# First MLP layer: a fourth pair of raw weight buffers, and the end of its first stage in written order

## The chip, the cores and the metric

The kernel runs on one core of a Trainium2 chip. The core has five engines with a queue of instructions each: PE (TensorE, matrix products), DVE (VectorE), ACT (ScalarE), POOL (GpSimd) and SP (SyncE, which here only issues transfers); POOL issues transfers too. The metric is the device time of the kernel in microseconds (us), the median of several runs. A change of under 0.2% of it, about 2 us, is not told from no change here.

## The reference, cut to what matters

The program works on x of 2048 tokens by 640 channels: four blocks one after the other, a spectral filter, a token MLP, the same filter again, the same MLP again.

```
def _B_ref(x, w1, b1, w2, b2):                 # w1 2048 x 1728, w2 1728 x 2048
    h = _layernorm(x, axis=-1)
    u = jnp.einsum("bsd,sf->bdf", h, w1) + b1
    u = _gelu(u)
    y = jnp.einsum("bdf,fs->bds", u, w2) + b2
    return y transposed to (b, s, d)

x = A_x
x = x + _A_ref(_layernorm(x), A_w_r, A_w_i)    # rfft2, times w_r + i w_i, irfft2
x = x + _B_ref(_layernorm(x), B_w1, B_b1, B_w2, B_b2)
x = x + _A_ref(_layernorm(x), A_w_r, A_w_i)
x = x + _B_ref(_layernorm(x), B_w1, B_b1, B_w2, B_b2)
```

## The kernel before, in words

`run` calls, twice, the spectral block (`a1`, `a2`) and an MLP: `b1st` the first time, `b2nd` the second. The change lies in `b1st` (lines 929 to 1166), the first MLP, and in one number set in `setup` (line 134).

**Precision.** Products are in float16 with each operand split into a high and a low part. A weight tile `raw` (float32) gives `wh` (ACT, a scaled copy) and `wl` (DVE, the rest); `h` is `hh` and `hl`, `u` is `uh` and `ul`. A product is three: high by high, low by high, high by low. Before a weight tile can be split its scale must be known: ACT reads the tile once and sums squares (`scan1`, the `junk<-raw` instructions), DVE reduces (`sqb`), PE adds over the partitions with a product by ones (`total`, a one-column matmul into `ps`), and some six one-column DVE operations make a power of two (`scale1`; `step(m)` runs the next piece of it).

**First stage.** A loop over `ft` = 0 to 13 (line 1008); the text calls one turn product `ft`. Each makes a tile of u, 128 features by 640 channels, from 16 blocks `j` of h; its weights are tile `m = ft`, taken in the order `SEQ`. From `ft` = 2 on a product is 96 matmuls of 320 columns, `both` (line 997). After it comes the gelu (lines 1060 to 1075): ACT writes `t` and `q` from the accumulator, DVE makes `q`, ACT takes the tanh, DVE writes `uf[i]`, the float32 u. `uh` and `ul` are made from `uf` by `usplit` (line 980, two DVE operations), which needs `su`, the scale of u, set by `scale_u` in product 11 at `j` = 8. Before the change the first six parts are spread over product 12, the next six over product 13, and the last two follow at the end (lines 1057 to 1059, 1076 and 1077).

**Second stage.** A loop over 16 rows `j` (line 1105), weight tiles m = 14 to 29. A row is 82 matmuls over the 14 tiles of u in the order `SEQ`; the last six of them read `uh[12]` and `ul[12]`, the last tile made. The result is added to a row of x (`xt`, loaded by `load`), written back, normalised and folded for the next spectral block, whose first products (`a0_s1`, `ps<-tM,fh` and `ps<-tM,fl`) lie between the rows.

**Weight pipeline.** While product or row m runs, these are issued (m counted through both stages): `wload(m + 3)` on SP, two transfers of half a tile each; `wstore(m)` and, in the first stage, sums of tiles (`wsum`, `wssplit`), kept for the second MLP and issued from POOL; `wsplit(m + 1)` (ACT `wh`, DVE `wl`, two halves); `scan1(m + 3)` and the steps of its scale. The raw tiles go in turn into `nr` = 3 pairs of buffers: `wr[max(m - 2, 0) % nr]`, in the pools `wraw`, `wr` and `wr2` (line 866). So the load of tile m + 3 goes into the buffers of tile m and waits until `wl` of m and the sums with it have read them. The split parts have two sets of buffers (`wp[m % 2]`), so `wh` of m + 2 waits until the product of m is done.

**Order.** A planner puts the instructions of each engine in an order of its own, by its own estimates of when each can start; the engines then run in that order. While `self.pin` is true, an instruction that goes through the wrappers of `Pin` (line 49: DVE, ACT, POOL's computing, PE) is tied behind the one written before it on the same engine. Transfers issued by `nc.sync` and `nc.gpsimd` are not tied. In `b1st` only lines 939 to 949 and the last row of the second stage (lines 1124 to 1153) are pinned before the change.

**Memory.** Pools lie on two stacks from the two ends of the on-chip memory, left and right; a tile put where a closed pool lay waits for the last reader of the tiles it covers. After the first stage `uf`, `b1`, `h` and `ha` are closed and the pools of the second stage's spectral tables (`tD`, `tM`, `tS2`, `tI2`) and rows (`xt`) are opened there.

## Time and profile before

| what | value |
|---|---|
| median of 3 runs | 1017.25 us (1016.85 to 1018.95) |
| the profiled execution's own time | 1017.07 us |
| its span, first to last instruction | 1015.3 us |
| PE busy | 969.4 us, 95% |
| DVE busy | 781.8 us, 77% |
| ACT busy | 576.5 us, 57% |
| POOL busy | 300.0 us, 30% |
| mean granted PE clock | 0.979 |

Times in the profile are counted from the first instruction. Almost all compute instructions carry line 59, the line of the `Pin` wrapper that issues them, so they are told apart by the names of their tiles: `ps<-hl,wh` is a matmul with `hl` moving and `wh` as weights. A row of a timeline has the start, the time from start to end of the group, the engine, the line, the operation, output and inputs, the shape and the count; in square brackets stand the idle time before it and what ended that. A row of waits has the waiting engine and tile, the releaser, the total in us, how often, and the longest. In tables by stretch each engine has its busy time and, in brackets, its instruction count; PEclk is the granted clock of PE as a share of full speed, and the last two columns are the share of time the DMA engines were busy and the GB/s they moved.

The first stage of the first MLP lies from about 184 us (first products of `both_high`) to 367 us, its second stage from 367 to about 567 us.

### The profile page before, as it was taken

The numbers are of one execution on the slowest core, as the hardware profiler recorded it, in microseconds if no ns is written. First come the engines' busy times: TensorE is split into PE (matmuls) and PEld (weight loads), VectorE is DVE, ScalarE is ACT, GpSimd is POOL, SyncE is SP. The second block draws the span as 40 slices with busy tenths as digits, with TensorE's granted clock in tenths as the row PEclk, the third lists the DMA queues.
The fourth block names the chain that finished last, engine by engine and source line by source line (L and its number), as shares of the span: only waits on it lengthen the run. The fifth ranks groups of instructions, "written<-read, shape, count | busy, mean of one in ns | idle before, by whom it ended". The sixth has DMA issues, their size and how long they took to land.

```text
span 1015.3 us, 20992 instructions
## 1 busy us (share of the span) xinstructions
PE 969.4 (95%) x8235; PEld 721.2 (71%) x8235; DVE 781.8 (77%) x1493; ACT 576.5 (57%) x890; POOL 300.0 (30%) x502
## 2 busy tenths in 40 slices
PE   4889999999999999999999799999999999999998
PEld 3778777677777667777777688776777777677776
DVE  7978978988777784666666689789965557998885
ACT  5857668687666455555553377685643454544531
POOL 6937857412212201222222277574000000000000
PEclk9599999999999999999999999999999999999999
DMA  7865356557657546464423455365444446755411
GB/s 232 279 185 164 115 178 219 206 187 255 236 195 250 186 124 246 139 193 146 126 89 117 126 181 181 105 229 204 159 156 164 145 142 228 245 177 190 153 45 53
DMA packets 67259, 176.45 MB, mean 174 GB/s; under 512 B 7996, under 2 KB 15320, under 8 KB 67160
## 3 DMA queue, kind: packets, MB, share of 16 engines
q1 hardware_dynamic: 59384, 146.92, 45.1%
q0 software_dynamic: 7776, 28.20, 7.5%
q8 instruction: 64, 1.05, 0.4%
q14 instruction: 35, 0.29, 0.1%
HBM read 127.24 MB, written 47.84 MB: 172 GB/s over the span
## 4 chain that ended last, share of the span: by engine, by line
PE 36%; DVE 13%; ACT 6%; POOL 3%; issue 3%; DMA 2%; SPq 0%; ACTq 0%; DVEq 0%; POOLq 0%
PE ps L59 36%; DVE wl L59 3%; DMA xt<-x 2%; DVE st L59 2%; DVE xt L59 1%; POOL eo L59 1%; DVE f L59 1%; ACT wh L59 1%; ACT xt L59 1%; ACT z L59 1%; DVE s1l L59 1%; ACT junk L59 1%; POOL xt L59 1%; DVE Yl L59 1%; DVE S L59 1%
## 5 line engine op out<-in xcount | busy, mean ns | idle before, releaser
L59 PEld LDWEIGHTS <-wh 128*128 128x128 f16 x2602 | 251.9, 98 | 103.6 <-issue 5.0
L59 PEld LDWEIGHTS <-wl 128*128 128x128 f16 x1610 | 157.5, 98 | 66.0 <-DVE wl L59 2.8
L59 PE MATMUL ps<-ul,wh 128*128 128x320 f16 x448 | 133.9, 301 | 0.6 <-DVE ul L59 0.6
L59 PE MATMUL ps<-uh,wl 128*128 128x320 f16 x448 | 133.9, 301 | 0.1
L59 PE MATMUL ps<-uh,wh 128*128 128x320 f16 x416 | 124.8, 300 | 1.6 <-DVE s L59 1.6
L59 PE MATMUL ps<-hl,wh 128*128 128x320 f16 x496 | 102.2, 299 | 0.9 <-DVE hl L59 0.9
L59 PEld LDWEIGHTS <-wo 128*128 128x128 f16 x756 | 73.9, 98 | 29.4 <-DVE wo L59 0.8
L59 DVE SCALAR_TENSOR_TENSOR wl<-raw,s,wh 128x896 f16<-128x896 f32 (+2 forms) x64 | 75.0, 1176 | 12.9 <-ACT wh L59 12.7
L59 ACT ACTIVATE junk<-raw 128x896 bf16<-128x896 f32 (+1 forms) x60 | 59.5, 991 | 44.2 <-DMA raw<-w 44.0
L59 POOL TENSOR_TENSOR r<-v,mh 128x1 f32<-128x1 f32 x64 | 36.4, 569 | 158.4 <-DVE nm L59 149.0
L59 PE MATMUL ps<-tDi,Yh 128*128 128x322 f16 x320 | 71.3, 300 | 0.2
L59 DVE TENSOR_TENSOR f<-eo 128x256 f32<-128x256 f32 (+1 forms) x124 | 39.1, 368 | 40.7 <-POOL eo L59 40.1
L59 ACT ACTIVATE wh<-raw,s 128x896 f16<-128x896 f32 (+2 forms) x68 | 67.2, 1010 | 2.3 <-DVE s L59 1.6
L59 POOL TENSOR_TENSOR xt<-xt,ec 128x320 f32<-128x320 f32 x64 | 52.5, 842 | 34.2 <-DVE xt L59 34.0
L59 ACT ACTIVATE z<-xt,nb,r 128x640 f32<-128x640 f32 x31 | 28.5, 919 | 57.6 <-POOL z L59 45.3
L59 PE MATMUL ps<-ph,tS 128*128 128x321 f16 (+2 forms) x288 | 58.5, 286 | 1.3 <-DVE tb L59 1.3
L59 PE MATMUL ps<-u,wo 128*128 128x320 f16 x420 | 59.0, 299 | 0.5 <-DVE wo L59 0.5
L59 DVE BATCH_NORM_STATS2 st<-xt 128x6 f32<-128x320 f32 x126 | 55.3, 480 | 5.2 <-DMA xt<-x 4.5
L59 PE MATMUL ps<-hha,wh 128*128 128x320 f16 x288 | 58.1, 299 | 0.9 <-DVE wh L59 0.9
L59 POOL TENSOR_TENSOR eo<-z 128x320 f32<-128x320 f32 x62 | 53.3, 881 | 17.0 <-ACT z L59 15.1
L59 PE MATMUL ps<-tM,f 128*128 128x128 f32 x160 | 39.5, 426 | 19.6 <-DVE f L59 19.6
L59 PE MATMUL ps<-tDi,Yl 128*128 128x322 f16 x192 | 55.7, 299 | 1.7 <-DVE Yl L59 1.7
(251 smaller groups left out, 2376.6 us busy)
## 6 DMA issues: line engine op xcount, KB each, us to landing
xt<-x SPq DMA_DIRECT2D x79, 320.0 KB
raw<-w SPq DMA_DIRECT2D x32, 512.0 KB
w<-w SPq DMA_DIRECT2D x48, 321.0 KB
x<-xt SPq DMA_DIRECT2D x47, 320.0 KB
raw<-w SPq DMA_DIRECT2D x32, 448.0 KB
raw<-w2z SPq DMA_DIRECT2D x32, 448.0 KB
w1S<-sp POOLq DMA_DIRECT2D x20, 512.0 KB, 3.7
out<-xt SPq DMA_DIRECT2D x15, 320.0 KB
```

Source lines behind the costliest of these rows:

```text
L59: i = f(*a, **k)
```

## The change

There are now four pairs of raw buffers: `nr` is 4, a pool `wr3` is opened beside `wr` and `wr2`, tiles 3, 4 and 5 are loaded ahead of the loop, and product or row m loads tile m + 4. The scan of a tile stays where it was written.

From the end of product 11's matmuls to the end of the first stage (`ft >= NFT - 3`) the instructions are pinned in written order: the gelu of product 11, all of products 12 and 13 with their gelus, and the last parts of u.

The 14 parts of u (`usplit`, now taken in turn by `nextu`) are spread anew: two beside each of the last three gelus (one after `q`'s ACT write, one after the tanh), three in each of the products 12 and 13 (`j` = 6, 9, 12), two at the end.

```
-        self.second, self.nr = False, 3
+        self.second, self.nr = False, 4
...
-        self.wr[1:3] = (self.push(a, side=self.sp) for a in ("wr", "wr2"))
+        self.wr[1:] = (self.push(a, side=self.sp) for a in ("wr", "wr2", "wr3"))
...
-        for m in (3, 4):
+        for m in (3, 4, 5):
             self.wload(m)

         def ahead(m, w):

-            if m + 3 < NFT + NJ:
-                self.wload(m + 3)
+            if m + 4 < NFT + NJ:
+                self.wload(m + 4)
...
+        todo = iter(SEQ)
+
+        def nextu():
+            i = next(todo)
+            usplit(i, uf[i])
...
-                    if ft >= NFT - 2 and 1 < j < 14 and j % 2 != ft % 2:
-                        i = SEQ[(j - 2) // 2 + 6 * (ft - NFT + 2)]
-                        usplit(i, uf[i])
+                    if ft >= NFT - 2 and j in (6, 9, 12):
+                        nextu()
+            self.pin = ft >= NFT - 3
             dup, i = ft == 1, SEQ[ft]
...
             T.activation(q, pv, AF.Square, scale=c1, bias=bb)
+            if ft >= NFT - 3:
+                nextu()
             V.scalar_tensor_tensor(q, q, 1.0 / GC, t, op0=ALU.add, op1=ALU.mult)
             T.activation(q, q, AF.Tanh, scale=GS * GC)
+            if ft >= NFT - 3:
+                nextu()
             V.scalar_tensor_tensor(uf[i], q, 1.0, t, op0=ALU.add, op1=ALU.mult)
-        for k in SEQ[12:]:
-            usplit(k, uf[k])
+        nextu()
+        nextu()
+        self.pin = False
...
+        self.pop("wr3")
         self.pop("wr2")
```

## The prediction

> **What bounds the kernel now.** I read first how busy the engines are by stretch: the first stage from product 2 on, then the second stage once its first row is through.

> ```profile
> 207.00:367.00 160.00, 157.79 (x1171) 113.20 (x1169) 127.61 (x222) 105.63 (x139) 34.52 (x63) 1.00 0.63 216
> 382.00:557.00 175.00, 174.86 (x1415) 128.46 (x1414) 107.33 (x303) 89.77 (x131) 36.27 (x84) 1.00 0.47 148
> ```

> PE (first pair of numbers) is busy in 157.8 of 160 us and in 174.9 of 175. Only PE's gaps can be won. The waits of PE between 207 and 382 us are four:

> ```profile
> PE ps L59 <- DVE wl L59: 1.7, 1, 1.7
> PE ps L59 <- DVE s L59: 1.6, 1, 1.6
> PE ps L59 <- DVE ul L59: 0.6, 1, 0.6
> PE ps L59 <- DVE sqb L59: 0.5, 1, 0.5
> ```

> PE's timeline places the first three, and the windows give the clock beside them:

> ```profile
> 352.25 0.43 PE L59 MATMUL ps<-hl,wh 128*128 128x320 f16 x2
> 354.36 0.45 PE L59 MATMUL ps<-hha,wl 128*128 128x320 f16 x2 [1.67 <-DVE wl L59]
> ```
> ```profile
> 366.89 0.30 PE L59 MATMUL ps<-uh,wh 128*128 128x320 f16 x1
> ...
> 377.10 0.30 PE L59 MATMUL ps<-uh,wl 128*128 128x320 f16 x1
> 379.05 0.30 PE L59 MATMUL ps<-uh,wh 128*128 128x320 f16 x1 [1.65 <-DVE s L59]
> 379.97 0.43 PE L59 MATMUL ps<-ul,wh 128*128 128x320 f16 x1 [0.62 <-DVE ul L59]
> ...
> 383.23 0.30 PE L59 MATMUL ps<-ul,wh 128*128 128x320 f16 x1
> ```
> ```profile
> 352.00:354.00 2.00, 0.69 (x6) 0.28 (x3) 2.00 (x5) 0.00 (x0) 1.23 (x1) 1.00 0.11 47
> ```
> ```profile
> 380.00:382.00 2.00, 2.00 (x8) 1.14 (x8) 0.21 (x1) 0.79 (x1) 0.00 (x0) 0.50 1.04 426
> ```

> The 76 matmuls from 366.89 to 377.10 are 75 steps in 10.21 us, 0.136 us a matmul; a product of 96 is then 13.06 us. Product 13 stops after two pairs for its `wl` (354.36). The second stage begins at 366.89 and stops after 377.10 for the last tile of u, twice (for `uh`, which ended at 378.99, and for `ul`; the `s` named in the first wait is a small operation that ran just behind `uh`), and then runs at clock 0.50. Why is the last u late? The chain of waits, followed back from the end, passes there:

> ```profile
> 373.93 0.77 ACT t L59
> 374.70 0.79 ACT q L59
> 375.51 0.90 DVE q L59 x2
> 376.52 1.15 DVE wl L59
> 377.67 0.73 DVE uf L59
> 378.47 0.52 DVE uh L59
> 379.06 0.86 DVE ul L59
> ```
> ```profile
> 382.22 8.62 DMA xt<-x
> 390.86 0.84 ACT xt L59
> ```
> ```profile
> ACT junk L59 <- DMA raw<-w: 42.7, 21, 3.8
> ```
> ```profile
> 368.75 0.95 ACT L59 ACTIVATE junk<-raw 128x896 bf16<-128x896 f32 x1 [2.02 <-DMA raw<-w]
> ```

> Product 13 was done when 366.89 began, but ACT starts its gelu at 373.93: ACT goes in order, and ahead of `t` stand the scans of a later tile, waiting for their load (2.02 here; 42.7 between 207 and 382 us, up to 3.8 at once). SP issues such a load only when `wl` of an older tile has freed its buffer. So load, scan, `wh`, `wl`, load is a ring that runs just in time, and each gelu trails its product.

> **The parts, one by one.**

> *Fourth pair.* A tile is loaded one product (13.06 us) earlier against its scan. The longest wait, 3.8 us, fits three times over, so the 42.7 us on ACT go, and ACT can start a gelu when its product ends. Bytes and instructions stay; SP's loads are the same, each behind an older `wl`. The one new early load, tile 5, is behind tiles 3 and 4 in the same queue, and the DMA engines then stand idle:

> ```profile
> 202.00:204.00 2.00, 1.63 (x11) 1.06 (x11) 1.72 (x8) 0.59 (x1) 0.00 (x0) 1.00 0.00 0
> ```

> I cost it at nothing; if that cover is missing, tile 3's scale is later, and PE's wait for `sqb` (0.5, above) grows. That wait is the bound both ways: 0.5 won or about as much lost.

> *Parts of u moved.* In the middle of product 12 DVE ran parts back to back and only then `wl` of product 13:

> ```profile
> 350.45 1.67 DVE L59 SCALAR_TENSOR_TENSOR ul<-uf,su,uh 128x640 f16<-128x640 f32 x2
> 352.11 1.00 DVE L59 TENSOR_SCALAR uh<-uf,su 128x640 f16<-128x640 f32 x2
> 353.03 1.27 DVE L59 SCALAR_TENSOR_TENSOR wl<-raw,s,wh 128x1024 f16<-128x1024 f32 x1
> ```

> A part is (1.67 + 1.00)/2 = 1.34 us. In written order product 12's slot holds the gelu of product 11 with two parts, then both `wl` (`j` = 2 and 4), then three parts: 5 x 1.34 + q and uf 1.63 + two `wl` 2.5 = 10.8 us of DVE in 13.06. `wl` is done 1.56 (t and q, below) + 0.90 + 1.34 + 0.73 + 2.5 = 7.0 us into product 12, six before it is wanted. Won: 354.36 - (352.25 + 2 x 0.136) = 1.84 us.

> *The end of the stage.* Call T the end of product 13. DVE and ACT then need: t and q 1.56 (a part beside them), DVE q 0.90, a part 1.34 (longer than the tanh beside it), uf 0.73, two parts 2.68: the last u is ready at T + 7.2. PE asks for it after 76 matmuls, at T + 10.3. Both stops go: 379.05 - 377.24 = 1.81, and 379.97 - 379.19 = 0.78. With them goes the slow clock: 13 steps took 3.26 us from 379.97 to 383.23 where 13 x 0.136 = 1.77 would do; 1.49.

> What is late next? `wl` of row 1's tile: its buffer is free only at T, DVE has it done by T + 7.2 + 2 x 1.15 = T + 9.5 if all of it queues behind the parts, and row 1 starts after 82 matmuls, at T + 11.15. The small scale operations share the 1.65 left. Bounds: nothing, or a stop like the 1.84 above; I take nothing.

> *The pinned order.* Its added wait: PE's one-column sums, tied at `j` = 4 and 10, hold every matmul behind them until DVE has reduced a scan. Between 0 and the 0.5 of the `sqb` row; I take 0, since the scans no longer wait. On ACT the scans of product 13 stand ahead of its gelu, now for tiles loaded a product earlier. POOL's queue has one tied memset; nobody waits for it before row 0.

> **Does the second stage pass the gain on?** Its rows are nearly bound by a second thing:

> ```profile
> 405.31 0.30 PE L59 MATMUL ps<-uh,wh 128*128 128x320 f16 x1
> 513.34 0.30 PE L59 MATMUL ps<-uh,wh 128*128 128x320 f16 x1
> 525.55 0.30 PE L59 MATMUL ps<-uh,wh 128*128 128x320 f16 x1
> 537.76 0.30 PE L59 MATMUL ps<-uh,wh 128*128 128x320 f16 x1
> ```
> ```profile
> 520.07 1.03 ACT junk L59 x2
> ...
> 526.72 28.77 PE ps L59 x229
> ```

> From 405.31 to 513.34 PE makes nine rows of 12.00; the next two take 12.21. In the chain of waits no step is PE's from 377 to 526.72: it runs over ACT, DVE, POOL and transfers. Its second-stage part starts when the first `xt` lands (390.86), gains no time, and has caught PE up at 513: 2 x 0.21 = 0.42 lost. So PE's gain arrives only if the first `xt` comes earlier by as much. It was issued 2.3 us after the last `ul` (379.92) and landed 8.62 later. With T = 366.89 - 1.84 = 365.05 the last u is at 372.25, and by the same intervals `xt` lands at 383.2, 7.7 us earlier. That exceeds PE's gain, so the 0.42 goes too.

> Sum: 1.84 + 1.81 + 0.78 + 1.49 + 0.42 = 6.34 us. The profiled execution took 1017.07, its span 1015.3; it becomes 1010.7. The median, 0.18 above it, becomes 1010.9. Two microseconds, 0.2%, is about what can be told from no change.

> [...] The 1.84 gap left the clock at 1.00; 1.81 and 0.78, one matmul apart, were followed by 0.50. [...]

> **Rivals.**

> *One: the chain starts no earlier.* SP may still issue the loads of the second stage behind raw loads that wait for row 1's `wl`, which hangs on T. Before, `xt` landed 390.86 - 366.89 = 24.0 after T; kept, it lands at 389.0, 1.84 earlier, and the chain, which decides at the end, gives 1015.4. For it: the chain ran for eleven rows without PE. Against: it now has the last u 7.7 us earlier, and one raw tile less to wait for.

> *Two: the slow clock is not owed to the gap* and stays: 1010.9 + 1.49 = 1012.4. For it: the 1.84 gap did nothing. Against: 0.50 begins right behind the stop.

> *Three: something of the gain is eaten by the bounds above* (a stop of up to 1.84 at row 1, 0.5 at a sum, some of the chain): 1012 to 1014.

> *Four, slower: the rows get a longer chain.* The planner orders the second stage anew, since raw tiles come earlier; if one more scan (1.03, the `junk` step) comes to stand in each row's chain, eleven rows to 526 pay 11.3. Less 6 us of earlier start that is 5.3 slower, 1022.5. It decides from 0.73 us a row on. For it: the chain is already the slower of the two by 0.21. Against: scans stand in it already, as at 520.07, and have more freedom now.

> **Chances.** The forecast 0.53 (1010 to 1012.3), two 0.05, three 0.14, one 0.13, four 0.15. Faster by over 0.2% (below 1015.2): 0.53 + 0.05 + 0.14 = 0.72. Same: 0.13, rival one at 1015.4. Slower: 0.15. The range reaches from 1009.9 (the forecast less the `sqb` wait and as much again at the start) to 1017.0, past rival one, and leaves out rival four and a little below.

> **What would show it.** ACT's waits for `raw` near zero; `t` of product 13 within 1 us of its last matmul; no stop at the first `wl` of product 13 nor at the last `ul`; clock 1.00 through both stages; the first `xt` landed within 19 us of T; row spacing 12.0 to the end. I am wrong if PE gets new waits for `wl` in the second stage, or stops at a sum.

## The result and the profile after

The changed kernel took 1011.89 us (median of 5 runs, 1010.04 to 1012.57), the kernel before 1017.25 (median of 5, 1016.5 to 1018.95). The ratio is 0.9936, with a 95% interval of 0.9923 to 0.9948: 6.5 us faster, between 5.3 and 7.8 (the two medians differ by 5.4). The profiled execution took 1010.95 against 1017.07, its span 1009.1 against 1015.3. A second set of runs of the same two kernels (further down) gave 1012.70 against 1017.94, ratio 0.9955 [0.9938, 0.9972], 4.6 us faster.

The stretches first, as before: from product 2 on, then the second stage once its first row is through (busy time of PE, PEld, DVE, ACT and POOL, granted clock, share of DMA, GB/s).

```profile
207.00:365.00 158.00, 157.29 (x1169) 113.02 (x1167) 127.87 (x227) 108.20 (x144) 32.74 (x63) 1.00 0.64 223
380.00:551.00 171.00, 171.00 (x1395) 126.39 (x1393) 104.23 (x301) 86.05 (x123) 36.21 (x84) 1.00 0.44 141
```

PE is busy in 157.3 of 158 us and in all of 171.0. Its waits between 207 and 382 us, four in the kernel before, are one kind, and ACT's waits for raw tiles are about half of what they were:

```profile
PE ps L59 <- DVE sqb L59: 0.7, 2, 0.5
```
```profile
ACT junk L59 <- DMA raw<-w: 22.4, 12, 3.0
```

PE's timeline: the second stage begins 1.65 us earlier (366.89 before), the last part of u costs a step of 0.32 instead of 0.136, and the rows that started at 405.31, 513.34, 525.55 and 537.76 start here:

```profile
365.24 0.30 PE L59 MATMUL ps<-uh,wh 128*128 128x320 f16 x1
...
375.59 0.30 PE L59 MATMUL ps<-uh,wh 128*128 128x320 f16 x1
375.91 0.30 PE L59 MATMUL ps<-ul,wh 128*128 128x320 f16 x1
...
399.75 0.30 PE L59 MATMUL ps<-uh,wh 128*128 128x320 f16 x1
507.76 0.30 PE L59 MATMUL ps<-uh,wh 128*128 128x320 f16 x1
519.79 0.30 PE L59 MATMUL ps<-uh,wh 128*128 128x320 f16 x1
531.79 0.30 PE L59 MATMUL ps<-uh,wh 128*128 128x320 f16 x1
```

From 387.75 to 531.79 the rows are 12.00 to 12.03 apart. The chain of waits passes the end of the first stage as before, only earlier:

```profile
374.47 0.46 DVE uh L59
...
375.00 0.86 DVE ul L59
...
375.88 9.19 DMA xt<-x
...
385.10 0.84 ACT xt L59
```

ACT and DVE at the end of product 13 do not look as predicted:

```profile
364.51 0.95 ACT L59 ACTIVATE junk<-raw 128x896 bf16<-128x896 f32 x1 [2.83 <-issue]
...
365.58 0.95 ACT L59 ACTIVATE junk<-raw 128x896 bf16<-128x896 f32 x1
...
366.53 1.03 ACT L59 ACTIVATE wh<-raw,s 128x896 f16<-128x896 f32 x1
367.47 0.87 ACT L59 ACTIVATE t<-ps,b1s,c 128x640 f32<-128x640 f32 x1
```
```profile
367.59 1.15 DVE L59 SCALAR_TENSOR_TENSOR wl<-raw,s,wh 128x896 f16<-128x896 f32 x1 [1.79 <-PE ps L59]
...
370.41 1.15 DVE L59 SCALAR_TENSOR_TENSOR wl<-raw,s,wh 128x896 f16<-128x896 f32 x1
```

Two scans and a `wh` of later tiles stand ahead of `t`, which starts 2.2 us after the product's end, and two `wl` stand between the steps of the gelu on DVE. The first of these scans waits 2.83 us, for which this profile names no releaser. In run e7 (below) ACT has the same work here, and there it is named:

```profile
364.46 0.95 ACT L59 ACTIVATE junk<-raw 128x896 bf16<-128x896 f32 x1 [2.82 <-DVE sqb L59]
```

So this wait is for a sum on DVE and not for a load. By the count of scans it is the scan for row 1 (tile 18). The kernel keeps the sums of squares in two `sq` tiles in turn, so this scan can write only once `sqb` of tile 16 has read the one it needs, and the pin ties that `sqb` behind the parts of u in product 13. The link over `sq` is read from the kernel; no run changes it.

Where did the 6.2 us of span come from? Four distances cut it up. The first stage, from the last stop for `hl` near 203 us (202.94 before, 202.91 after) to T, the start of the second stage: 163.95 to 162.33, 1.62 won. From T to the twelfth row start counted from 405.31 and 399.75, called row 12 here and in the expectations: 170.87 to 166.55, 4.32 won. From there to the first product with `tD` behind the last row:

```profile
571.34 0.31 PE L59 MATMUL ps<-tD,s1h 128*128 128x160 f16 x2 [0.39 <-ACT s1h L59]
```
```profile
564.65 0.32 PE L59 MATMUL ps<-tD,s1h 128*128 128x160 f16 x2 [0.45 <-ACT s1h L59]
```

33.58 to 32.86, 0.72 won. From there to the end 443.96 to 444.45, 0.49 lost again. 1.62 + 4.32 + 0.72 - 0.49 = 6.17, and 0.03 from the start. In a second pair of profiles (a1 and a2 below) the same four distances give 0.46, 4.24, 1.11 and 1.83, and 1.41 from the start: only the 4.3 of the second stage repeats.

### The profile page after: what moved, and what is told of

It is laid out like the page before. It is cut to its first block, busy times and chain, and to the rows that moved or that the text cites. A ratio compares the mean times of both kernels' runs of the same rounds, so it can differ in the third digit from the quotient of the medians.

```text
span 1009.1 us, 20992 instructions
## 1 busy us (share of the span) xinstructions
PE 966.7 (96%) x8235; PEld 720.8 (71%) x8235; DVE 781.1 (77%) x1493; ACT 577.0 (57%) x890; POOL 297.9 (30%) x502
## 4 chain that ended last, share of the span: by engine, by line
PE 48%; DVE 22%; ACT 12%; POOL 8%; issue 6%; DMA 4%; SPq 0%; ACTq 0%; DVEq 0%; POOLq 0%
PE ps L59 48%; DVE wl L59 3%; POOL eo L59 3%; DVE f L59 3%; DMA xt<-x 2%; DVE st L59 2%; DVE xt L59 2%; ACT junk L59 2%; ACT z L59 2%; ACT wh L59 2%; POOL xt L59 2%; DVE s1l L59 1%; DVE Yl L59 1%; ACT xt L59 1%; DVE hl L59 1%
## 5 line engine op out<-in xcount | busy, mean ns | idle before, releaser
L59 PEld LDWEIGHTS <-wh 128*128 128x128 f16 x2602 | 251.4, 98 | 101.3 <-issue 3.1
L59 PEld LDWEIGHTS <-wl 128*128 128x128 f16 x1610 | 157.5, 98 | 62.2 <-issue 1.0
L59 PE MATMUL ps<-ul,wh 128*128 128x320 f16 x448 | 133.1, 299 | 0.0
L59 PE MATMUL ps<-uh,wl 128*128 128x320 f16 x448 | 133.1, 299 | 0.0
L59 PE MATMUL ps<-uh,wh 128*128 128x320 f16 x416 | 124.3, 299 | 0.0
L59 PE MATMUL ps<-hl,wh 128*128 128x320 f16 x496 | 102.3, 299 | 0.9 <-DVE hl L59 0.9
L59 PEld LDWEIGHTS <-wo 128*128 128x128 f16 x756 | 73.9, 98 | 29.4 <-DVE wo L59 0.8
L59 DVE SCALAR_TENSOR_TENSOR wl<-raw,s,wh 128x896 f16<-128x896 f32 (+2 forms) x64 | 75.1, 1177 | 22.5 <-ACT wh L59 19.6
L59 POOL TENSOR_TENSOR r<-v,mh 128x1 f32<-128x1 f32 x64 | 36.3, 567 | 162.1 <-DVE nm L59 152.6
L59 ACT ACTIVATE junk<-raw 128x896 bf16<-128x896 f32 (+1 forms) x60 | 59.5, 992 | 27.6 <-DMA raw<-w 24.4
L59 PE MATMUL ps<-tDi,Yh 128*128 128x322 f16 x320 | 71.3, 300 | 0.2
L59 ACT ACTIVATE wh<-raw,s 128x896 f16<-128x896 f32 (+2 forms) x68 | 67.1, 1010 | 6.0 <-DVE s L59 5.5
L59 DVE TENSOR_TENSOR f<-eo 128x256 f32<-128x256 f32 (+1 forms) x124 | 39.0, 368 | 40.6 <-POOL eo L59 40.1
L59 POOL TENSOR_TENSOR xt<-xt,ec 128x320 f32<-128x320 f32 x64 | 52.4, 841 | 34.0 <-DVE xt L59 33.9
L59 ACT ACTIVATE z<-xt,nb,r 128x640 f32<-128x640 f32 x31 | 28.5, 919 | 57.0 <-POOL z L59 45.2
L59 PE MATMUL ps<-ph,tS 128*128 128x321 f16 (+2 forms) x288 | 58.5, 286 | 1.3 <-DVE tb L59 1.3
L59 PE MATMUL ps<-u,wo 128*128 128x320 f16 x420 | 59.0, 299 | 0.5 <-DVE wo L59 0.5
L59 DVE BATCH_NORM_STATS2 st<-xt 128x6 f32<-128x320 f32 x126 | 55.3, 481 | 5.2 <-DMA xt<-x 4.5
L59 PE MATMUL ps<-hha,wh 128*128 128x320 f16 x288 | 58.1, 299 | 0.9 <-DVE wh L59 0.9
L59 POOL TENSOR_TENSOR eo<-z 128x320 f32<-128x320 f32 x62 | 53.3, 880 | 17.1 <-ACT z L59 15.1
L59 PE MATMUL ps<-tM,f 128*128 128x128 f32 x160 | 39.5, 426 | 19.6 <-DVE f L59 19.6
L59 PE MATMUL ps<-tDi,Yl 128*128 128x322 f16 x192 | 55.7, 299 | 1.5 <-DVE Yl L59 1.5
```

The costliest lines, as they stand in the source:

```text
L59: i = f(*a, **k)
```

## The experiments

Two theories at the start. **R**: the fourth pair did it, by loosening the ring of load, scan, `wh`, `wl` that holds up ACT. **O**: the order did it, the pinning and the new places of the parts. All runs in one table; the medians are over 5 to 12 runs, the ratio is to runs of the kernel before on the same chip (1017.81, 1017.47 and 1017.94 for the three groups of experiments), the distances are those of the profiled execution, and "xt" is when ACT takes the first `xt`, counted from T.

| run | median us | ratio [95%] | first stage | xt after T | row 12 after T | row 12 to `tD` | ACT's raw waits |
|---|---|---|---|---|---|---|---|
| before | 1017.25 | | 163.95 | 23.97 | 170.87 | 33.58 | 42.7 |
| a1, before again | 1017.42 | 1.0006 [0.9991, 1.0021] | 162.45 | 24.00 | 170.76 | 33.55 | 42.6 |
| after | 1011.89 | 0.9936 [0.9923, 0.9948] | 162.33 | 19.86 | 166.55 | 32.86 | 22.4 |
| a2, after again | 1012.70 | 0.9955 [0.9938, 0.9972] | 161.99 | 19.75 | 166.52 | 32.44 | 23.1 |
| e1, pair only | 1014.53 | 0.9967 [0.9955, 0.9979] | 162.33 | 22.83 | 169.35 | 32.79 | 40.3 |
| e2, order only | 1012.79 | 0.9953 [0.9939, 0.9967] | 162.11 | 20.95 | 167.76 | 33.53 | 31.8 |
| e3, no pin | 1014.47 | 0.9970 [0.9957, 0.9983] | 161.98 | 22.91 | 169.45 | 32.78 | 39.1 |
| e4, parts at old places | 1012.97 | 0.9953 [0.9940, 0.9967] | 161.99 | 22.64 | 170.67 | 32.23 | 23.8 |
| e5, last u 1.5 late | 1013.80 | 0.9969 [0.9959, 0.9980] | 162.43 | 19.62 | 168.12 | 32.23 | 22.5 |
| e6, last u 3.0 late | 1014.90 | 0.9980 [0.9965, 0.9995] | 162.26 | 20.55 | 168.75 | 32.24 | 24.5 |
| e7, xt later | 1012.19 | 0.9952 [0.9936, 0.9968] | 162.62 | 22.71 | 166.63 | 32.82 | 24.2 |
| e8, five pairs | 1013.61 | 0.9957 [0.9940, 0.9974] | 164.77 | 20.14 | 166.53 | 31.63 | 11.8 |
| e9, e1 with xt first | 1012.79 | 0.9956 [0.9942, 0.9971] | 162.50 | 15.82 | 167.54 | 32.23 | 42.6 |
| e10, after with xt first | 1010.50 | 0.9929 [0.9915, 0.9943] | 162.99 | 15.16 | 166.53 | 32.24 | 24.4 |

The intervals of e1 to e5 and a2 overlap, so the medians hardly rank the variants. The argument rests on the distances to row 12, of one profile each; in both kernels that were profiled twice, that distance repeated to 0.11 us.

### Which part of the change

**e1, the fourth pair alone** (the diff's pinning and `nextu` left out):

```
-        self.second, self.nr = False, 3
+        self.second, self.nr = False, 4
...
-            if m + 3 < NFT + NJ:
-                self.wload(m + 3)
+            if m + 4 < NFT + NJ:
+                self.wload(m + 4)
```

> The fourth pair of buffers alone; pins and parts of u as before. If the ring of load, scan, wh and wl is the cause (theory R), ACT's waits for raw tiles fall by half or more, t of product 13 starts within 3 us of the last matmul of that product, the 2.6 us of stops for the last u and the slow clock behind them go, and the second stage keeps 12.0 us a row: 1011 to 1013.5, the upper end if the parts still push wl of product 13 back by 1.8. If the order on the engines is the cause (theory O), the waits for raw tiles go too, but the cluster of parts still stands ahead of wl of product 13 and the last u stays late: 1014 to 1017.

ACT's waits for raw hardly fall, the stop at the first `wl` of product 13 is gone, the slow clock is not there (from T to the row at 402.08 it is 35.57 us, 38.42 in the kernel before and 34.51 in the changed one), and yet the kernel wins only 3 us. The rows say why:

```profile
ACT junk L59 <- DMA raw<-w: 40.3, 19, 4.6
```
```profile
389.34 2.38 ACT L59 ACTIVATE xt<-xt,b2s 128x640 f32<-128x640 f32 x3 [6.86 <-DMA xt<-x]
```
```profile
402.08 0.30 PE L59 MATMUL ps<-uh,wh 128*128 128x320 f16 x1
414.08 0.30 PE L59 MATMUL ps<-uh,wh 128*128 128x320 f16 x1
...
523.86 0.30 PE L59 MATMUL ps<-uh,wh 128*128 128x320 f16 x1
```

One row of 12.00, and then nine in 109.78 us, 12.20 each, which is the pace of the chain over ACT, DVE, POOL and transfers that the kernel before showed from 513 on. PE came to the second stage earlier, but the first `xt` landed at T + 22.8, and the chain caught PE up at the second of these rows. This is the prediction's rival one, nearly as it was worked out there (1015.4). Neither theory had all its signs right: `t` of product 13 starts 5.6 us after its product and the waits for raw stay, against R, and the late `wl` of product 13 that O expected is gone.

**e2, the order alone** (three pairs):

```
-        self.second, self.nr = False, 4
+        self.second, self.nr = False, 3
...
-            if m + 4 < NFT + NJ:
-                self.wload(m + 4)
+            if m + 3 < NFT + NJ:
+                self.wload(m + 3)
```

> The pinned order and the new places of the parts alone, with three pairs of buffers. Theory R: the scans still wait for their loads, in pinned order ahead of the gelus, so t of product 13 starts some 5 us or more after its product and the stops for the last u stay: 1015 to 1017. Theory O: wl of product 13 comes before the parts and frees the buffers early, the ring has slack in products 12 and 13 without a fourth pair: 1011 to 1012.5.

Most of the gain is there: 4.8 us by the ratio, with `t` of product 13 3.2 us behind its product. Small stops remain, and `xt` is 1.1 us later than in the changed kernel:

```profile
367.47 0.18 PE L59 MATMUL ps<-sqb,ones 128*128 128x1 bf16 x1 [0.39 <-DVE sqb L59]
376.53 0.30 PE L59 MATMUL ps<-ul,wh 128*128 128x320 f16 x1 [0.41 <-DVE ul L59]
```

With the fourth pair these go too; in the profiles that is 1.2 us at row 12 and 0.7 to 1.1 behind it, while the medians (1012.79 against 1011.89 and 1012.70) do not settle it.

**e3, the changed kernel without the pinning**:

```
-            self.pin = ft >= NFT - 3
```

> The changed kernel without the pin; four pairs and the new places of the parts stay. Theory R: the planner has what it needs, 1011 to 1012.5, no stop of PE above 0.5 between 207 and 380 us. Theory O: without the tie the planner runs the parts ahead of wl of product 13 or ahead of DVE's gelu operations again: a stop of 1 to 2 us, 1013 to 1016.

It ends where e1 does: raw waits 39.1, the first `xt` at T + 22.9, rows of 12.20 (and one of 13.02, in which PE stops for 0.32 and 0.35). The stop of 1 to 2 us at the end of the first stage that theory O expected did not come, only its time did. So the pair and the new places of the parts do not bring the tail of the stage forward without the pinning.

**e4, pair and pinning, the parts at their old places**:

```
-                    if ft >= NFT - 2 and j in (6, 9, 12):
+                    if ft >= NFT - 2 and 1 < j < 14 and j % 2 != ft % 2:
                         nextu()
...
-            if ft >= NFT - 3:
-                nextu()
```

> Four pairs and the pin, the parts of u at their old places (six in product 12, six in 13, two at the end). If the new places are worth nothing beside the other two edits: 1010.5 to 1012, as the changed kernel, the last u ready about a part (1.3 us) earlier after the last product since no part stands beside its gelu. If they are worth something: six parts (8 us) beside the gelu and wl overfill product 12 or 13 and a wl or a sum comes late, a stop of 0.5 to 2 us, 1012 to 1014.

Here PE stops for a sum in the first row, whose reduction stands behind the late parts on DVE, and the clock falls behind that stop (369.16 to 372.57 us at 0.50):

```profile
369.44 0.18 PE L59 MATMUL ps<-sqb,ones 128*128 128x1 bf16 x1 [2.66 <-DVE sqb L59]
```

Row 12 comes at T + 170.67, the 166.5 of the undisturbed kernel plus 2.66 and the 1.49 of the prediction for a slow stretch (170.7). The first `xt` is late too (T + 22.6). Without the slow stretch, which by the slot theory (below) hangs on how the stop lies in slots of 3.41 us, the chain would still hold row 12 at 22.64 + 146.7 = 169.3 (the next section has the 146.7). So in these profiles the pinning moves row 12 by the full amount only with the parts at their new places, and theory O holds in this form: the two together first, the pair as their smaller complement. By the medians e2 and e4 are alike (0.9953 both).

### What sets the second stage

Where the chain decides, row 12 comes at a fixed distance from the first `xt`: 537.76 - 390.86 = 146.90 in the kernel before, 146.76 in a1, 146.52 in e1, 146.81 in e2, 146.54 in e3. Where PE decides, it comes at T + 166.53 plus PE's stops. The later of the two is the rule of the table. Three runs test it.

**e9, e1 with the first rows of x ahead of the tables** in SP's queue (one table, `tD`, still goes out first, at 375.20):

```
-        for q in range(4):
-            self.a0_load_m(q)
-        self.a0_load()
         p = self.pT
...
         xts = [load(0), load(1)]
+        for q in range(4):
+            self.a0_load_m(q)
+        self.a0_load()
```

> The fourth pair alone (no pinning, parts of u at their old places), with the first two rows of x issued ahead of the tables tM, tS2 and tI2. In the fourth pair alone the first xt was issued at 380.0 and landed at 389.3, rows were 12.2 apart from 414 to 524, and row 12 came at 535.86. Here xt is issued at about 379.5 and, with less ahead of it in the queues, lands at about 383 to 385. Chain theory: rows 12.0 apart, row 12 at 534.1, and 1.8 us faster than the fourth pair alone (about 1012.7 against 1014.5). Rival (12.2 a row is owed to the order of the rows' instructions, not to the landing): rows stay at 12.2 and the time at 1014.5.

```profile
377.01 0.80 SPq L1092 DMA_DIRECT2D xt<-x  x2
```
```profile
381.17 0.83 ACT L59 ACTIVATE xt<-xt,b2s 128x640 f32<-128x640 f32 x1 [1.76 <-DMA xt<-x]
```
```profile
532.89 0.30 PE L59 MATMUL ps<-uh,wh 128*128 128x320 f16 x1
```

The first `xt` is there 4.2 us after its issue instead of 9.3, all rows are 12.00 apart, row 12 comes at T + 167.54 (166.53, the two stops of 0.25 and 0.62 that were left for the last u, and 0.14 more), and the median is 1012.79 against 1014.53 for e1. So the rows of 12.20 go away with the late landing. The edit also changes the order of some steps of the first rows on ACT and DVE, so this run alone does not separate landing and order.

**e10, the same edit on the changed kernel**:

> The changed kernel with the first two rows of x issued ahead of the tables tM and tI2. From row 12 to the first product with tD at the end of the stage it took 32.9 us in the changed kernel (32.8 with the first xt put off, or with the fourth pair alone) and 32.23 where the chain had more room (the fourth pair alone with xt first). Chain theory: rows stay at 12.00, and this last stretch becomes 32.2: 0.6 us faster than the changed kernel. Rival (the chain has room enough in the changed kernel): no change.

```profile
533.86 0.30 PE L59 MATMUL ps<-uh,wh 128*128 128x320 f16 x1
...
566.10 0.31 PE L59 MATMUL ps<-tD,s1h 128*128 128x160 f16 x2 [0.37 <-ACT s1h L59]
```

32.24 from row 12 to `tD`, as expected; against the two profiles of the changed kernel (32.86 and 32.44) that is 0.2 to 0.6 us. Its first stage has two small stops, 0.47 for a sum and 0.18 for a `wl`, and is 0.66 longer than the changed kernel's. It is the fastest of the study, 1010.50 (1009.51 to 1011.86), 0.9929 against 0.9955 for the changed kernel on the same chip. The intervals overlap, so that it is better than the changed kernel is likely and not settled.

**e7, the first xt later** (one table loaded twice, xt issued behind it):

```
         self.a0_load()
+        twice = nc.sync.dma_start(self.tI2, A["tI2"])
...
-        xts = [load(0), load(1)]
+        with self.after(twice):
+            xts = [load(0), load(1)]
```

> The changed kernel with one table of the second stage (tI2) loaded twice, and the first rows of x issued behind the second load: PE's work is untouched, only the first xt lands later, by an estimate between 388 and 393 us instead of 385.1. Chain theory (from the landing of the first xt to the start of row 12 the chain over ACT, DVE, POOL and transfers takes 146.7 to 146.9 us, as in the kernel before and in the run with the fourth pair alone): rows 12.2 apart until that chain is through, row 12 at the landing + 146.8, so 535 to 540 instead of 531.8, and the kernel 3 to 8 us slower by just that. Rival (the second stage is PE's alone and rows of 12.2 have another cause): rows 12.0, 0 to 0.5 us slower.

```profile
387.90 0.83 ACT L59 ACTIVATE xt<-xt,b2s 128x640 f32<-128x640 f32 x1 [0.38 <-DMA xt<-x]
```
```profile
531.82 0.30 PE L59 MATMUL ps<-uh,wh 128*128 128x320 f16 x1
```

A miss. The landing came 2.8 us later, and row 12 only 0.03 later, 143.9 us behind it: no 3 to 8 us. The chain does catch PE up, in a row of 12.11 from 507.71 to 519.82, but it is some 2.8 us shorter here. The edit also put the raw loads of a later tile ahead of `xt`, and the first two rows' steps run in another order; which of the two shortens the chain is not separated. So 146.7 is a distance of this order of work and not a property of the landing.

### The length of a stop and the clock

**e5 and e6** put two and four idle operations ahead of the last part of u (four here; the results of the kernel are not touched):

```
         nextu()
+        for _ in range(4):
+            V.scalar_tensor_tensor(q, q, 1.0, t, op0=ALU.add, op1=ALU.mult)
         nextu()
         self.pin = False
```

> The changed kernel with two idle DVE operations of about 0.75 us each put ahead of the last part of u, so that this part is ready 1.5 us later (they rewrite q, which nobody reads any more; the result is unchanged). In the changed kernel PE asks for the last u at 375.59 and has it at 375.91. Here both theories expect two stops with one matmul between, about 0.85 us for uh and 0.8 for ul, 1.6 to 1.7 in all. Theory G (a stop of about 2 us or more is what lowers the clock): 1.7 is no more than the 1.67 that left the clock at 1.00 before, so 1.00 stays, and the kernel is 1.5 us slower than the changed one. Theory H (any stop at the start of the second stage lowers the clock, or the drop belongs to the place and not to the length): clock 0.50 for some 3 us after it, and 3.0 us slower. [...]

> The same with four such operations, so that the last part of u is ready 3.0 us later: stops of about 2.4 and 0.8 us with one matmul between. Theory G expects the clock at 0.50 for about 3 us behind the stops, which costs another 1.5 us, so 4.5 us slower than the changed kernel. If the drop has another cause than the gap, the clock stays at 1.00 and it is 3.0 slower. The first xt waits for the last ul, so it lands 3 us later too, at about 388; by the chain theory row 12 then starts at 388 + 146.8 = 534.9, no later than PE itself is, and nothing is added. [...]

e5 stops for 0.83 and 0.62 us, its clock stays at 1.00 (376.40 to 383.23 us), and row 12 is 1.6 us later against T than in the changed kernel: as theory G expected. e6 is a miss: PE took other matmuls of the row first, so the stop was one of 2.14 us,

```profile
377.69 0.43 PE L59 MATMUL ps<-uh,wh 128*128 128x320 f16 x2 [2.14 <-DVE uh L59]
```

and the clock stayed at 1.00, though the kernel before fell to 0.50 after 1.65 and 0.62, 2.27 in all. The length need not be what tells them apart. Behind the first 100 us the slow stretches of the kernel before last 3.41 us (379.63 to 383.05 and 567.36 to 570.77; a third, from 1014.5 us on, is cut short by the end of the program), that of the changed kernel too (560.56 to 563.97), that of e5 (560.72 to 570.96) three times as long, and in e6 the three slots from 560.28 to 570.52 are at 0.50. (Before, the three stretches of 2 us from 378 on have the clocks 0.91, 0.50 and 0.74, so 0.09 x 4 + 2.00 + 0.26 x 4 = 3.40 us are at 0.50.) Laid on a grid of 3.41 us, with the phase that each execution's own slow stretches give, they fill whole slots. The slots of the kernel before, then e4, e6 and a1:

```profile
352.32:355.74 3.42, 1.75 (x14) 1.04 (x13) 3.42 (x5) 0.67 (x1) 0.91 (x1) 1.00 0.33 93
376.22:379.63 3.41, 1.48 (x10) 0.81 (x9) 3.38 (x9) 1.93 (x4) 0.00 (x0) 1.00 0.64 176
379.63:383.05 3.42, 3.08 (x12) 1.77 (x12) 0.72 (x4) 1.84 (x3) 0.00 (x0) 0.50 0.99 370
560.53:563.95 3.42, 1.64 (x13) 0.96 (x10) 2.59 (x8) 0.81 (x2) 1.62 (x4) 1.00 0.00 0
563.95:567.36 3.41, 0.28 (x2) 0.11 (x2) 3.13 (x12) 0.90 (x3) 1.35 (x2) 1.00 0.25 96
567.36:570.77 3.41, 2.97 (x28) 2.90 (x28) 1.94 (x4) 1.08 (x4) 0.00 (x0) 0.50 0.36 96
```
```profile
365.75:369.16 3.41, 1.03 (x8) 0.51 (x6) 3.17 (x10) 2.19 (x3) 0.00 (x0) 1.00 0.00 0
369.16:372.57 3.41, 3.13 (x13) 1.82 (x14) 3.41 (x9) 2.74 (x5) 0.00 (x0) 0.50 0.12 14
```
```profile
375.96:379.37 3.41, 1.68 (x12) 1.15 (x12) 2.60 (x6) 0.02 (x1) 0.00 (x0) 1.00 0.92 264
379.37:382.78 3.41, 3.41 (x28) 2.46 (x27) 2.35 (x5) 1.96 (x2) 0.00 (x0) 1.00 1.05 411
```
```profile
376.87:380.28 3.41, 1.91 (x13) 1.26 (x13) 2.02 (x7) 1.38 (x3) 0.00 (x0) 1.00 0.83 272
380.28:383.69 3.41, 3.41 (x28) 2.47 (x26) 1.90 (x3) 2.57 (x4) 0.00 (x0) 1.00 0.89 274
```

The first pair of numbers is PE's. Idle for 3.41 - 1.48 = 1.93 us of a slot (before, 376.22), or 2.38 (e4), and the next slot is at 0.50; idle for 1.67, 1.78, 1.73 or 1.50, and it stays at 1.00. The 2.14 us of e6 lay across two slots.

**a1 and a2, both kernels once more**, the first of them a test of this:

> The kernel before once more, to see what two sets of runs of one kernel differ by, and for a second look at the clock. All slow stretches of the profiles so far lie on a grid of 3.41 us, whose phase differs from execution to execution, and behind the first 100 us a slot of the grid runs at 0.50 only when PE was idle for 1.93 us or more in the slot before (1.77 us never did it). Slot theory: the last-u stop comes again with about 1.65 and 0.62 us of idling; the clock drops behind it only if some 1.9 us of that lie in one slot of the grid, which is so for roughly half of the phases. Theory G (the length of the stop decides alone): 0.50 behind it in every execution. The time: 1.000 times that of before, to about 0.0015.

```profile
377.75 0.30 PE L59 MATMUL ps<-uh,wh 128*128 128x320 f16 x1 [1.34 <-DVE s L59]
378.66 0.30 PE L59 MATMUL ps<-ul,wh 128*128 128x320 f16 x1 [0.62 <-DVE ul L59]
```
```profile
536.65 0.30 PE L59 MATMUL ps<-uh,wh 128*128 128x320 f16 x1
```

The stop for the last u is there, a little shorter, with 1.50 us in one slot, and the clock stays at 1.00: the slot theory fits, and theory G with its bound of about 2 us does not. What the stops alone do not rule out is a bound on all the idling of a stop, between the 2.14 us of e6 and the 2.27 of the kernel before. What speaks for the slots is the grid, and that the same work near 55 us, ahead of the changed part, is followed by a slow slot in seven of the fourteen profiles (in before, after and e5 with 1.50 us of idling in the slot ahead of it). The stop at the first `wl` of product 13 was 0.28 us in this execution instead of 1.67. And yet row 12 comes at T + 170.76, as in the first profile, where PE lost more. That is the chain: the first `xt` was again at T + 24.0.

> The changed kernel once more, beside the kernel before on the same chip: 1011 to 1012.5, 5 to 7 us faster; PE waits between 207 and 382 us for sqb alone (0.5 to 0.8 in all); rows of 12.00; no slow clock between 100 and 550 us, since no slot of the grid has 1.9 us of idling there.

As expected in PE's waits, the rows and the clock. The median of 1012.70 lies just above the expected range, and by the ratio the gain is 4.6 us and not 5 to 7. The profiled span was 1006.9.

### Five pairs

**e8** takes the fourth pair one further (`nr` = 5, `wload(m + 5)`, a pool `wr4`, tiles 3 to 6 ahead of the loop):

```
-        self.second, self.nr = False, 4
+        self.second, self.nr = False, 5
```

> The changed kernel with five pairs of raw buffers, tiles 3 to 6 loaded ahead of the loop. Theory R (the raw ring is what the fourth pair loosened): ACT's waits for raw, 22.4 us between 207 and 382 in the changed kernel, fall by half or more again; what PE can still win by it is the waits that are left there, 0.2 us for the last ul and 0.17 for a sum, so 0 to 0.4 us faster. Theory O (the written order did it): waits for raw go on as they are, since the planner looks further ahead by as much, and the time is the same. Rival: a tile more to load at the start of the stage delays the sums (the sqb wait of 0.55 grows) or the first xt, and it is up to 1 us slower.

ACT's raw waits fall to 11.8, as theory R said and theory O did not. Yet `t` of product 13 starts 2.2 us after its product as before, behind the same scans. And nothing is won: PE now stops for `wl` in two products where it never did,

```profile
275.32 0.45 PE L59 MATMUL ps<-hha,wl 128*128 128x320 f16 x2 [1.21 <-DVE wl L59]
```

and for 0.76 at 302.46. The first stage takes 164.77, some 2.4 us more, and the last stretch 31.63, some 1 us less; the median is 1013.61. No run shows what reorders the two products.

## Why the prediction was right, and where it was not

**The time.** 1010.9 was forecast, with the sum 6.34 against the profiled execution; that one went from 1017.07 to 1010.95, 6.12 less. By distance the sum had 1.84 for the first stage (measured 1.62) and 1.81 + 0.78 + 1.49 + 0.42 = 4.50 for the second (4.32), nothing for the end of the second stage (0.72 won) and nothing behind it (0.49 lost). That the sum met this one pair of profiles to 0.22 us is in part luck: in the second pair the first stage gave 0.46 and behind the last u there was no slow clock to lose. The second set's 1012.70 lies in the range of rival three.

**The signs.** Three came: no stop at the first `wl` of product 13 and nearly none for the last u, the clock at 1.00 (from 100 to 550 us; near 560 us a slow slot stays, 560.56 to 563.97 at 0.50), rows of 12.0. Three did not: ACT's waits for raw tiles, `t` within 1 us, and the first `xt` within 19 us of T (19.86). PE also has one new stop for a sum in the first profile, of 0.17.

**The stop at the first `wl` of product 13** went, in every run that has any part of the change. But it is not a constant of the kernel before: 1.67 us in one of its executions and 0.28 in the other. A term read from one execution was the size of that execution.

**"A tile is loaded one product earlier ... so the 42.7 us on ACT go, and ACT can start a gelu when its product ends."** This step failed. The pair alone leaves 40.3, pair and order together 22.4, and `t` of product 13 starts 2.2 us after its product, behind the scans of a later tile and a `wh`. With a tile more in the ring the planner puts the scans of one tile more ahead of `t`: 38 half scans since the start, in e1 as in the changed kernel, against 36 in the kernel before and in e2. In the changed kernel the first of them then waits for `sqb`, 2.83 us. So a deeper ring does not cure it (e8, with five pairs, has `t` as late), and where these scans are not ahead (e4, 36) `t` starts 0.2 us after its product. The working named the scans ahead of the gelu and gave them no price.

**The end of the stage.** The last u was to be ready at T + 7.2 and was at 375.86, T + 10.6: the 2.2 us of `t`, and a `wl` of 1.15 that slipped between the pinned steps, which I had put behind all parts (a second one, at 367.59, ran while DVE had to wait for ACT's `q` anyway). The margin against PE's demand at T + 10.3 was 3.1, and all of it was used; a stop of 0.19 is what remained. Rival three describes this; it cost those 0.19.

**The slow clock** went from both profiles of the changed kernel, as forecast, since PE has no stop there. That the stop of 2.6 us brings it on every time, which the full 1.49 assumed, is wrong: by the slot theory it hangs on how the stop lies in the 3.41 us slots, and of two executions of the kernel before one had it (1.93 us of idling in one slot) and one had not (1.50, a1). Rival two fell: in e4 the drop came behind the new stop instead, and with no stop there was none.

**Who owns the 4.3 us of the second stage.** I added up PE's stops and asked of the chain only that it start early enough. Row 12 is the later of T + 166.5 + PE's stops and the first `xt` + 146.7. Before, PE's own time was 166.53 + (1.81 - 0.19) + 0.78 + 1.49 = 170.4, since 166.53 holds the 0.19 that remained, and the chain's was the measured 170.87: the chain decided, by the 0.4 that the prediction had found. So a gain in PE's stops alone would have been lost, as a1 shows, where PE loses some 1.8 us less and row 12 stays at 170.76. A gain in `xt` alone could have brought no more than those 0.4. In e1 row 12 won 1.5, the stops being gone and `xt` 1.1 earlier against T; in e4 `xt` was 1.3 earlier and a new stop ate it. The forecast held because the change moves both by some 4.1 us: the first `xt` landed 5.8 us earlier, 4.1 of it against T. I had said 7.7, with the last u 3.4 earlier than it was. After the change the two are tied, 166.5 against 19.86 + 146.7 = 166.6, and 0.2 to 0.6 us of the chain are still to be had at the end, as e10 shows.

**Rival one** is a real mechanism, and what e1 and e3 end in (1014.5 in both). What it says of SP's order still holds: the first table goes out right behind a raw load, at 378.12 before, 376.40 in e1 and 372.02 after, and that load waits for a `wl`. After the change this is the `wl` that ended at 371.56, so the same `wl` that delayed the last u let the tables go; no run separates its two effects. **Rival four** did not come: the pace of a row in the chain stays at 12.20, in e1 and e3 with four pairs as before with three. Its price was too high by its own rows: with the 7.7 us of earlier start that the working had, 11.3 would have left 3.6 and not 5.3.

## What to carry to other kernels

When two paths run side by side at nearly the same pace, find for each the fixed distance from its own start to a late mark; a gain on one is worth only what the other leaves, and a table of the two over a few runs shows which one decides. A deeper ring need not shorten waits if an order planned ahead uses the room to place its work earlier (42.7 to 40.3 us here); tie the few steps that feed the next stage, and look at what can still slip in between. And issue the first rows that a stage needs ahead of tables that it needs later: here that edit alone brought row 12 forward by 1.8 us where the chain decided (169.35 to 167.54).

## What the runs showed of the hardware

```profile
563.69:567.11 3.42, 2.77 (x23) 2.19 (x22) 1.71 (x3) 1.46 (x3) 0.00 (x0) 0.50 0.18 71
567.11:570.52 3.41, 3.41 (x28) 3.41 (x27) 0.47 (x1) 0.44 (x1) 0.00 (x0) 0.50 1.00 347
570.52:573.93 3.41, 3.41 (x35) 2.70 (x33) 1.88 (x4) 1.15 (x2) 0.00 (x0) 1.00 0.55 146
```

So stops of nearly one length cost different times, which the slot theory puts down to the phase. Behind the stop of 4.48 us in e10, which ended at 562.56, the matmuls were at full pace again by 566.10; behind the one of 4.47 us in e9, which ended at 561.59, they stayed slow to 570.8 (the rows of `ps<-tD,s1h` 0.40 us apart instead of 0.21). At this long stop near 560 us, which all these kernels have, the distance from the first product with `tD` to the first with `ph` was 3.98 us in the profiles of before, after, a2, e1, e2, e4 and e10, and 5.6 to 6.35 in those of a1, e3, e5, e6, e7, e8 and e9 (5.80 in e8, 6.35 in e9). This distance lies behind the first product with `tD`, which e7 and the changed kernel reach at 564.64 and 564.65, and e7's span is 2.1 us longer (1011.2 against 1009.1). One profiled span is not a verdict here to better than 2 us; the distance from T to row 12, ahead of that stop, repeated to 0.11 us.
